# Layer one's third feed-forward group by seven half-block products, and the input sums that these need in one run behind attention's last low part

## The chip, the cores and the metric

The kernel runs on one core of a Trainium2 chip. The metric is device time in microseconds (us) of one execution. The kernel before takes 616.91 us, the median of three runs (616.11, 616.91 and 617.58). A core has five engines with queues of their own that meet through semaphores: TensorE (PE in the profile, its weight loads PEld), VectorE (DVE), ScalarE (ACT), GpSimd (POOL) and SyncE (SP, which issues most of the DMAs here).

## What is computed

Three stages follow each other; all inputs are float32. Attention over 2 batches, 8 heads and 768 tokens (a local window, and 24 block summaries) gives `x` of 1536 tokens by 512. Then two feed-forward layers:

```python
h = x @ w_in                            # 1536 x 512 x 2048
x = (h / (1 + exp(-1.702 * h))) @ w_out # 1536 x 2048 x 512
gate = 1 / (1 + exp(-(x @ w_gate)))     # 1536 x 512 x 1536
val = x @ w_val
out = (gate * val) @ w_out2             # 1536 x 1536 x 512
```

## The kernel before

Both layers work on three token blocks of 512 (block 0, 1, 2) and on groups of 256 hidden features (two halves `f` of 128): eight groups in layer one, six in layer two. Each float32 operand of a matmul is kept as two parts, a high one rounded to the matmul's type and a low one with the rest (`xH`, `xL` for the tokens, `w..H`, `w..L` for weights, `gh`, `gl` for the gated hidden block). One product of such numbers takes three matmuls: low by high, high by low, high by high. A product over the 512 input features is so 12 matmuls of 128 x 128 by 512 columns, a half of it, over 256 features (`product`, L190), is 6.

A group has a first part (`x` by its columns of `w_in`, then the gate) and a second part (the gated block by its rows of `w_out`, `second`, L541: 24 matmuls for one token block in four quarters of six, each quarter added to an accumulator `acc` by VectorE, L575). The first part comes in three forms. `first` (L517) takes one token block straight, 2 x 12 matmuls at L489. `single` (L467) takes block 2 with half products at L197. `pair` (L402) takes blocks 0 and 1 together. There the two halves `f` and the two halves of the input features make a 2 by 2 matrix of weight blocks, the two halves of the features and the two token blocks a 2 by 2 matrix of token blocks, and their product is formed by seven block products in place of eight, in Strassen's way (Winograd's form). It needs four combinations of the weight blocks (made in `load`, L167 to L186, the tiles `ws` and `s..H`, `s..L`) and four of the token blocks (made once by `input_sums`, L248, the tiles `t1` to `t3`, and `t4`, which overwrites the low half of block 1's `xH` and `xL`). Products 5 and 6 are kept in SBUF by ScalarE (L428) and added to later ones by VectorE (L431).

`PAIRED = 3` says from which group on layer one uses `pair`. Groups 0 and 1 are done for blocks 0 and 1 inside attention, as a filler. Behind attention stand, one after the other with the second part of each step behind the first part of the next, the steps (group, block): (0, 2), (1, 2), (2, 0), (2, 1), (2, 2), (3, 2), and then `pair` of group 3, with `single` of group 4 behind it, and so on up to group 7.

Within that program order a scheduler places the instructions of each engine, except where `keep_in_program_order` holds them (the input sums do that on VectorE). The input sums are 14 VectorE instructions of 128 x 1024, handed out one by one while the steps run (`folding`). The first eight come from step (0, 2) on, the rest from step (2, 1) on. The first of them may not be placed before attention's last low part (`d_lo`, L783: `xL` of the last unit).

A weight piece of 1 MB passes through `load`: VectorE takes the words apart (`da`, `db`, L132), ScalarE rescales (`da<-da`, L140), VectorE joins (L150), ScalarE rounds to the high part (L155), VectorE subtracts to the low part (L157). Then follow, for pieces that `pair` reads, four small sums `ws` (L173), a cast (L182) and a subtraction (L184). A gated block is made by ScalarE's gelu (`sg`, L514) and cast (`gh`, L508), and GpSimd's subtraction (`gl`, L509).

Of the kernel before, what the change touches and what calls it, by code (L numbers as in the profile page):

```python
# [14 lines left out]
ALU = mybir.AluOpType  # L15
# [14 lines left out]
def attention_moe_moe2_kernel(ctx: ExitStack, tc: tile.TileContext, ins: dict, out: bass.AP):  # L30
# [5 lines left out]
    B, HP, _, S = vt.shape  # L36
# [13 lines left out]
    NTB = NT // TB  # L50
# [12 lines left out]
    xH, xL = [None] * NTB, [None] * NTB  # L63
# [36 lines left out]
    def drop(*key):  # L100
        w_free.extend(w_held.pop(key))
# [9 lines left out]
    def behind(a, b):  # L111

        tc.add_manual_dep(
            a.ins, b.ins.name,
            mybir.DependencyInfo(mybir.DependencyClass.NoSync, mybir.DependencyReason.DATA), reason="order",
        )

    def load(layer, g, i, early):
# [27 lines left out]

        after = [(1, PAIRED - 1, 2, m) for m in (0, 3)] if (layer, g, i) == (1, PAIRED + 1, 0) else []
        while after and after[0] not in added:
# [10 lines left out]
        yield  # L159
        if layer == 1 and (g < PAIRED or i == 1) or layer == 2 and i == 2:  # L160
            yield
# [26 lines left out]
    LO, HI = slice(0, KC // 2), slice(KC // 2, KC)  # L188
# [16 lines left out]
    steps = [(1, g, blk) for blk in range(2) for g in range(2)]  # L205
# [9 lines left out]

    mats = {1: [w_in, w_out], 2: [w_gate, w_val, w_out2]}
    pieces, weights, raws = [], {}, []
    PAIRED = 3
    wanted = [(1, g, i) for g in range(n1) for i in range(2)] + [(2, 0, i) for i in range(3)]
    for g in range(1, n2):  # L220
        wanted += [(2, h, i) for h, i in ((g, 0), (g - 1, 2), (g, 1)) if (h, i) != (0, 2)]
# [23 lines left out]
    def t_tile(name):  # L245
        return tp.tile([P, KC // 2, TB], F32R, tag=f"t{name}", name=f"t{name}")

    def input_sums():  # L248

        def tt(**x):
            ins = nc.vector.tensor_tensor(**x)
            tc.keep_in_program_order(ins)
            return ins

        f1, f2, f3 = (tp.tile([P, KC // 2, TB], F32, tag=f"f{n}", name=f"f{n}") for n in "123")
        h1, l1, h3, l3 = (t_tile(x) for x in ("1H", "1L", "3H", "3L"))

        def whole(to, blk, half):  # L260
            return tt(out=to, in0=xH[blk][:, half], in1=xL[blk][:, half], op=ALU.add)

        behind(whole(f1, 0, LO), live["lo"])
        yield
        whole(f3, 1, LO)
        yield
        tt(out=f1, in0=f3, in1=f1, op=ALU.subtract)
        yield
        whole(f2, 1, HI)
        yield  # L270
        tt(out=f3, in0=f2, in1=f3, op=ALU.subtract)
        nc.scalar.copy(h3, f3)
        yield
        tt(out=f2, in0=f2, in1=f1, op=ALU.subtract)
        nc.scalar.copy(h1, f1)
        yield
        tt(out=l3, in0=f3, in1=h3, op=ALU.subtract)
        yield
        tt(out=l1, in0=f1, in1=h1, op=ALU.subtract)
        yield  # L280
        h2, l2 = t_tile("2H"), t_tile("2L")
        h4, l4 = xH[1][:, LO], xL[1][:, LO]
        whole(f3, 0, HI)
        yield
        tt(out=f3, in0=f3, in1=f2, op=ALU.subtract)
        nc.scalar.copy(h4, f3)
        nc.scalar.copy(h2, f2)
        yield
        tt(out=l4, in0=f3, in1=h4, op=ALU.subtract)
        yield  # L290
        tt(out=l2, in0=f2, in1=h2, op=ALU.subtract)
        tsum.update({"1": (h1, l1), "2": (h2, l2), "3": (h3, l3), "4": (h4, l4)})
        yield
# [312 lines left out]
    with tc.manual_schedule(engines={mybir.EngineType.SP}), ExitStack() as es:  # L606
# [95 lines left out]
        live = {}  # L702
# [96 lines left out]
        for _ in range(4):  # L799
# [28 lines left out]
            out=win, in_=win, pattern=[[0, NSLOT], [1, P - W0]], compare_op=ALU.is_gt, fill=NEG,  # L828
# [3 lines left out]
            out=win, in_=win, pattern=[[0, NSLOT], [-1, P - W0]], compare_op=ALU.is_gt, fill=NEG,  # L832
# [64 lines left out]
    with tc.manual_schedule(engines={mybir.EngineType.SP}):  # L897
        places(6, "w_b")
        pool([gh_slots, gl_slots], GF + 1, "g_b")
        pool([sg_slots], 5, "sg_b")  # L900
        acc_b = ctx.enter_context(tc.tile_pool(name="acc_b", bufs=1, reuse_waits="tile"))
        tp = ctx.enter_context(tc.tile_pool(name="tp", bufs=1, reuse_waits="tile"))
        ps_a, ps_b = (
            ctx.enter_context(tc.tile_pool(name=f"ps_{x}", bufs=n, space=PSUM, reuse_waits="tile"))
            for x, n in (("a", 4), ("b", 2))
        )
        ps_f, ps_s = Slots("h", (ps_a, 4)), Slots("h", (ps_h, 2), (ps_b, 2))
        folding, sums_1 = iter(()), input_sums()

        def run(main, rest=iter(()), after=()):  # L910

            for n, _ in enumerate(main):
                pull(1)
                next(folding, None)
                for _ in range(after.count(n)):
                    next(rest, None)
            for _ in rest:
                pull(1)
                next(folding, None)

        def seconds(layer, g, *blks):
            for blk in blks:
                yield from second(layer, g, blk, g == ends[layer])

        steps = [(1, g, 2) for g in range(2)] + [(1, 2, blk) for blk in range(NTB)] + [(1, PAIRED, 2)]
        prev = None
        for step in steps:
            need((*step[:2], 0))
            run(first(*step))
            if step[2] == 2 and step[1] < PAIRED:  # L930
                drop(*step[:2], 0)
            if prev:
                need((*prev[:2], 1))
                run(second(*prev, False))
                if prev[2] == 2:
                    drop(*prev[:2], 1)
            if step == (1, 0, 2):
                folding = itertools.islice(sums_1, 8)
            elif step == (1, 2, 1):
                for _ in folding:  # L940
                    pass
                folding = sums_1
            prev = step
        top = n1 - 1

        LEAD = PAIRED + 1
        for g in range(PAIRED, n1):  # L950
            need((1, g, 0), (1, g, 0, "s"))
            for _ in folding:
                pass
            if g - 1 in (LEAD, top - 1):
                run(pair(1, g), seconds(1, g - 1, 1, 0), range(7))
                if g - 1 == LEAD:
                    drop(1, g - 1, 1)
            else:
                n = g if g <= LEAD else g - 1
                need((1, n, 1))  # L960
                run(pair(1, g), second(1, n, 2, False), (0, 2, 4, 5))
                if n < g:
                    drop(1, n, 1)
            drop(1, g, 0, "s")
            if g <= LEAD:
                drop(1, g, 0)
            need((1, g, 1))
            if g in (LEAD, top - 1):
                continue
            n = g + 1 if g < LEAD else min(g, top - 1)  # L970
            need((1, n, 0))
            run(single(1, n), seconds(1, g, 1, 0), (0, 0, 1, 1, 2, 2, 3, 3))
            if g < LEAD:
                drop(1, g, 1)
            else:
                drop(1, n, 0)
        folding = token_sums()
        run(single(1, top), second(1, top - 1, 2, False), range(4))
        drop(1, top, 0)
        drop(1, top - 1, 1)  # L980
        prev = (1, top)
        ps_f, ps_s = Slots("h", (ps_a, 4), (ps_b, 2)), Slots("h", (ps_h, 2))

        def ahead(g):
            if (2, g, 1, "s") not in weights:
                pull(1)

        for g in range(n2):
            need((2, g, 0), (2, g, 1), (2, g, 0, "s"), (2, g, 1, "s"))
            for _ in folding:  # L990
                pass
            rest = second(*prev, 2, prev[0] == 1)
            if g == 0:
                rest = itertools.chain(rest, half_sums())
            for slot, _ in enumerate(pair(2, g)):
                if g:
                    ahead(g + 1)
                elif slot > 4 and (2, 0, 2) not in weights:
                    pull(1)
                if slot % 2 or g == 0 and slot:  # L1000
                    next(rest, None)
                if g and slot % 4 == 3:
                    ahead(g + 1)
            for _ in rest:
                pass
            drop(*prev, prev[0])
            drop(2, g, 0, "s")
            drop(2, g, 1, "s")
            need((2, g, 2))
            rest = seconds(2, g, 0, 1)  # L1010
            for _ in halves(g):
                ahead(g + 1)
                next(rest, None)
                ahead(g + 1)
            for _ in rest:
                pass
            drop(2, g, 0)
            drop(2, g, 1)
            prev = (2, g)
        for _ in second(*prev, 2, True):  # L1020
            pass
# [40 lines left out]
```

## Time and profile before

| | |
|---|---|
| median of three runs | 616.91 us |
| the profiled execution, of it the span of the core | 616.49 us, 614.7 us |
| TensorE busy | 599.2 us (97%), 3348 matmuls |
| VectorE, ScalarE, GpSimd busy | 447.1 us (73%), 313.5 us (51%), 199.2 us (32%) |
| chain that ended last | PE 90%, DMA 8% |
| DMA | 58.10 MB, mean 95 GB/s |

The span runs from the first to the last instruction of the core. What lies around it, 616.49 less 614.7, is 1.79 us. The chain that ended last is followed back from the last instruction to what released it; where it runs along one engine, that engine had no free time there. A matmul's line in the timeline has a duration of 0.39 us, but matmuls overlap: what a matmul costs is the distance from its start to the start of the next.

### The profile page before, as it was taken

To read this page: it belongs to the slowest core of one execution; us is meant where nothing else is said; L and a number is where in the kernel's file an instruction comes from. 1 tells how busy PE (TensorE), PEld (TensorE's weight loads), DVE (VectorE), ACT (ScalarE), POOL (GpSimd) and SP (SyncE) were. 2 spreads that over 40 slices of the span, in tenths; PEclk is the share of its full clock that TensorE was granted. 3 is DMA by queue.
4 is the path that set the end of the run, shared out by engine and by line. 5 is a ranking of instruction groups with operands and counts; after the bars stand their busy time and mean duration, and the time that the engine had idled before them with its cause. 6 is when DMAs were issued, how large, how long until landed. Compare 5 with 4: busy or idle time off the path is not lost.

```text
span 614.7 us, 8764 instructions
## 1 busy us (share of the span) xinstructions
PE 599.2 (97%) x3348; PEld 498.3 (81%) x3348; DVE 447.1 (73%) x655; ACT 313.5 (51%) x620; POOL 199.2 (32%) x164
## 2 busy tenths in 40 slices
PE   7698999999999999999999999999999999999997
PEld 4576787788888888888888888898898898898896
DVE  6699665399929988877559889568759669777434
ACT  4788657566424645535345667635445246344230
POOL 6796685323331243413322021022022022122030
PEclk9999999999999999999999999999999999999999
DMA  9999653022301421331002023222222222100014
GB/s 301 336 297 331 234 138 70 1 70 69 136 1 68 138 68 69 101 106 60 9 0 70 0 69 101 105 69 69 69 69 69 68 69 70 68 2 1 0 51 155
DMA packets 25161, 58.10 MB, mean 95 GB/s; under 512 B 1568, under 2 KB 1824, under 8 KB 25120
## 3 DMA queue, kind: packets, MB, share of 16 engines
q1 hardware_dynamic: 24400, 56.24, 28.3%
q10 hardware_dynamic: 720, 1.31, 0.6%
q8 instruction: 26, 0.43, 0.3%
q14 instruction: 15, 0.12, 0.1%
HBM read 53.08 MB, written 3.15 MB: 91 GB/s over the span
## 4 chain that ended last, share of the span: by engine, by line
PE 90%; DMA 8%; DVE 0%; POOL 0%; SPq 0%; issue 0%; ACTq 0%; POOLq 0%
PE ps_o L489 37%; PE ps_y L197 16%; PE ps_x L197 10%; PE ps_v L197 10%; PE ps_h L489 8%; PE ps_h L197 4%; DMA q<-in_q 3%; PE ps_s L710 2%; DMA vt<-in_vt 2%; PE ps_x L762 2%; DMA vwin<-in_v 1%; DMA k<-in_k 1%; PE ps_p L743 1%; PE ps_s L708 0%; POOL kx L699 0%; POOL gl L509 0%
## 5 line engine op out<-in xcount | busy, mean ns | idle before, releaser
L509 POOL TENSOR_TENSOR gl<-sg,gh 128x512 fp32r<-128x512 f32 x84 | 125.6, 1501 | 377.2 <-ACT gh L508 290.0
L575 DVE TENSOR_TENSOR acc<-ps_o,acc 128x512 f32<-128x512 f32 x143 | 96.4, 684 | 66.5 <-PE ps_o L489 66.3
L489 PE MATMUL ps_o<-gl,w_1H 128*128 128x512 f32 x192 | 75.2, 393 | 0.3 <-POOL gl L509 0.3
L489 PE MATMUL ps_o<-gh,w_1H 128*128 128x512 f32 x192 | 74.7, 390 | 0.0
L489 PE MATMUL ps_o<-gh,w_1L 128*128 128x512 f32 x192 | 71.9, 395 | 1.5 <-ACT gh L508 1.4
L508 ACT CAST gh<-sg 128x512 fp32r<-128x512 f32 x84 | 51.6, 621 | 31.3 <-DVE sg L500 24.9
L489 PE MATMUL ps_o<-w_2L,gh 128*128 128x512 f32 (+1 forms) x146 | 56.6, 387 | 0.0
L489 PE MATMUL ps_o<-w_2H,gh 128*128 128x512 f32 (+1 forms) x146 | 56.4, 386 | 0.0
L489 PE MATMUL ps_o<-w_2H,gl 128*128 128x512 f32 (+1 forms) x146 | 56.3, 389 | 0.1
L150 DVE SCALAR_TENSOR_TENSOR da<-da,db 128x1024 uint32<-128x1024 uint32 x34 | 46.9, 1379 | 9.6 <-ACT da L140 9.0
L140 ACT ACTIVATE da<-da 128x1024 f32<-128x1024 f32 x34 | 36.1, 1061 | 24.1 <-DVE da L132 21.9
L489 PEld LDWEIGHTS ps_o<-gh,w_1L 128*128 128x128 f32 x192 | 35.9, 188 | 9.3 <-ACT gh L508 2.0
L489 PEld LDWEIGHTS ps_o<-gl,w_1H 128*128 128x128 f32 x192 | 36.1, 188 | 7.6 <-POOL gl L509 0.5
L489 PEld LDWEIGHTS ps_o<-gh,w_1H 128*128 128x128 f32 x192 | 36.1, 188 | 7.3
L699 POOL TENSOR_SCALAR kx<-k 128x384 f32<-128x384 f32 x24 | 33.0, 1375 | 20.0 <-DMA k<-in_k 10.9
L723 ACT ACTIVATE e<-ps_s,nm 128x128 f32<-128x128 f32 x96 | 34.3, 381 | 9.1 <-DVE nm L715 8.0
L489 PEld LDWEIGHTS ps_o<-w_2H,gh 128*128 128x128 f32 x146 | 27.4, 188 | 5.7
L489 PE MATMUL ps_h<-xL,w_0H 128*128 128x512 f32 x80 | 31.4, 393 | 0.3 <-DVE xL L783 0.3
L489 PEld LDWEIGHTS ps_o<-w_2L,gh 128*128 128x128 f32 x146 | 27.5, 188 | 5.1
L132 DVE TENSOR_SCALAR db<-raw 128x1024 uint32<-128x1024 uint32 x33 | 30.8, 933 | 1.1 <-DMA raw<-in_moe_w_out 0.7
L489 PEld LDWEIGHTS ps_o<-w_2H,gl 128*128 128x128 f32 x146 | 27.4, 188 | 5.2 <-DVE acc L575 0.3
L489 PE MATMUL ps_h<-xH,w_0L 128*128 128x512 f32 x80 | 31.5, 403 | 0.0
(244 smaller groups left out, 1482.1 us busy)
## 6 DMA issues: line engine op xcount, KB each, us to landing
raw<-in_moe_w_out SPq DMA_DIRECT2D x13, 1024.0 KB, 4.9
raw<-in_moe_w_in SPq DMA_DIRECT2D x8, 1024.0 KB, 7.5
raw<-in_moe_w_gate SPq DMA_DIRECT2D x6, 1024.0 KB, 5.0
raw<-in_moe_w_val SPq DMA_DIRECT2D x6, 1024.0 KB, 5.0
q<-in_q SPq DMA_DIRECT2D x20, 256.0 KB, 9.4
vwin<-in_v SPq DMA_DIRECT2D x6, 768.0 KB, 9.6
k<-in_k SPq DMA_DIRECT2D x8, 400.0 KB, 7.7
out<-acc SPq DMA_DIRECT2D x11, 256.0 KB, 2.0
```

Of the source, the lines that this page charges most:

```text
L132: ins = nc.vector.tensor_scalar(**x)
L140: nc.scalar.activation(af, af, AF.Prelu, scale=REBIAS, alpha=-2.0 ** 32)
L150: ins = nc.vector.scalar_tensor_tensor(out=a, in0=a, scalar=3, in1=b, op0=ALU.logical_shift_left, op1=ALU.bitwise_or)
L197: nc.tensor.matmul(ps, lhsT=a[x][:, kk, :], rhs=b[y][:, kk, :], start=start and i == 0, stop=i == n - 1, skip_group_check=True,)
L489: nc.tensor.matmul(ps, lhsT=a, rhs=b, start=i == 0, stop=i == n - 1)
L508: nc.scalar.copy(gh, sg)
L509: nc.gpsimd.tensor_tensor(out=gl, in0=sg, in1=gh, op=ALU.subtract)
L575: added[layer, g, blk, m] = nc.vector.tensor_tensor(out=a[:, m, :], in0=ps, in1=a[:, m, :], op=ALU.add)
L699: nc.gpsimd.tensor_scalar(out=to, in0=x, scalar1=scale, scalar2=None, op0=ALU.mult)
L710: nc.tensor.matmul(ps[:, j, :], lhsT=t[:, j, :], rhs=kt[:, j, :], start=False, stop=j == G - 1)
L723: nc.scalar.activation(e[:, j, :], s[:, j, :], AF.Exp, bias=nm[:, j:j + 1], accum_out=sm[:, j:j + 1])
L762: nc.tensor.matmul(ps[64 * e:64 * e + 64, j, :], lhsT=x[:, h * D:(h + 1) * D], rhs=y[:, j, 64 * e:64 * e + 64], start=n == 0, stop=n == le ...
```

## The change

`PAIRED` goes from 3 to 2. Group 2's blocks 0 and 1 are no longer computed by `first`; they are computed by `pair`, and the steps behind attention are (0, 2), (1, 2), (2, 2) and then `pair` of group 2, with the second part of (2, 2) in it, then `single` of group 3 with the second parts of group 2's blocks 1 and 0. `LEAD`, which moves the second part of block 2 in the loop, stays 4. The weight piece (2, 0) now gets its four sums too. The input sums come one after the other from step (0, 2) on, without the pause after eight, and each of the four that read `xH` and `xL` may not be placed before attention's last low part.

```diff
@@ -215,7 +215,7 @@
-    PAIRED = 3
+    PAIRED = 2
@@ -258,9 +258,9 @@
         def whole(to, blk, half):
-            return tt(out=to, in0=xH[blk][:, half], in1=xL[blk][:, half], op=ALU.add)
-
-        behind(whole(f1, 0, LO), live["lo"])
+            behind(tt(out=to, in0=xH[blk][:, half], in1=xL[blk][:, half], op=ALU.add), live["lo"])
+
+        whole(f1, 0, LO)
         yield
         whole(f3, 1, LO)
         yield
@@ -922,7 +922,7 @@
-        steps = [(1, g, 2) for g in range(2)] + [(1, 2, blk) for blk in range(NTB)] + [(1, PAIRED, 2)]
+        steps = [(1, g, 2) for g in range(2)] + [(1, PAIRED, 2)]
@@ -935,10 +935,6 @@
             if step == (1, 0, 2):
-                folding = itertools.islice(sums_1, 8)
-            elif step == (1, 2, 1):
-                for _ in folding:
-                    pass
                 folding = sums_1
             prev = step
@@ -946,7 +942,7 @@
-        LEAD = PAIRED + 1
+        LEAD = PAIRED + 2
```

TensorE, right behind the second part of step (1, 2), in the kernel before (`ps_o_1881` is the last quarter of that second part, `ps_h_1890` the first part of block 1 of group 2):

```order
L489 MATMUL ps_o_1881<-gh1_1_2_1_1749,w1_1_1H_849 128x512
L489 MATMUL ps_h_1890<-xH1_765,w1_2_0L_1680 128x512
L489 MATMUL ps_h_1890<-xL1_766,w1_2_0H_1679 128x512
L489 MATMUL ps_h_1890<-xH1_765,w1_2_0H_1679 128x512
L489 MATMUL ps_h_1890<-xH1_765,w1_2_0L_1680 128x512
L489 MATMUL ps_h_1890<-xL1_766,w1_2_0H_1679 128x512
L489 MATMUL ps_h_1890<-xH1_765,w1_2_0H_1679 128x512
```

The same place now (`ps_x_1904` is product 1 of group 2, `gh1_2_2_0` and `gl1_2_2_0` the gated block 2 of group 2, half 0):

```order
L489 MATMUL ps_o_1892<-gh1_1_2_1_1749,w1_1_1H_849 128x512
L197 MATMUL ps_x_1904<-xH0_321,w1_2_0L_1680 128x512
L197 MATMUL ps_x_1904<-xL0_322,w1_2_0H_1679 128x512
L197 MATMUL ps_x_1904<-xH0_321,w1_2_0H_1679 128x512
L197 MATMUL ps_x_1904<-xH0_321,w1_2_0L_1680 128x512
L197 MATMUL ps_x_1904<-xL0_322,w1_2_0H_1679 128x512
L197 MATMUL ps_x_1904<-xH0_321,w1_2_0H_1679 128x512
L489 MATMUL ps_o_1915<-gh1_2_2_0_1824,w1_2_1L_1804 128x512
L489 MATMUL ps_o_1915<-gl1_2_2_0_1825,w1_2_1H_1803 128x512
L489 MATMUL ps_o_1915<-gh1_2_2_0_1824,w1_2_1H_1803 128x512
L489 MATMUL ps_o_1915<-gh1_2_2_1_1847,w1_2_1L_1804 128x512
L489 MATMUL ps_o_1915<-gl1_2_2_1_1848,w1_2_1H_1803 128x512
```

The 24 matmuls of block 0 and the 24 of block 1 are gone from the first form; product 1 with 6 matmuls stands here, the other six products follow between the second parts, and the gated block 2 of group 2 is now read 126 matmuls behind the first one of step (0, 2).

VectorE, up to the piece (3, 0) being taken apart (`da` from `raw1_3_0`), in the kernel before:

```order
L253 TENSOR_TENSOR f2_1727<-f2_1727,f1_1726 128x1024
L157 TENSOR_TENSOR w1_2_1L_1776<-da_1773,w1_2_1H_1775 128x1024
L253 TENSOR_TENSOR t3L_1732<-f3_1728,t3H_1731 128x1024
L253 TENSOR_TENSOR t1L_1730<-f1_1726,t1H_1729 128x1024
L132 TENSOR_SCALAR da_1854<-raw1_3_0_1703 128x1024
L150 SCALAR_TENSOR_TENSOR da_1854<-da_1854,db_1855 128x1024
```

and now:

```order
L253 TENSOR_TENSOR t1L_1730<-f1_1726,t1H_1729 128x1024
L253 TENSOR_TENSOR f2_1727<-f2_1727,f1_1726 128x1024
L253 TENSOR_TENSOR t3L_1732<-f3_1728,t3H_1731 128x1024
L132 TENSOR_SCALAR db_1886<-raw1_3_0_1703 128x1024
L157 TENSOR_TENSOR w1_2_1L_1804<-da_1801,w1_2_1H_1803 128x1024
L253 TENSOR_TENSOR f3_1728<-xH0_321,xL0_322 128x1024
L253 TENSOR_TENSOR t2L_1864<-f2_1727,t2H_1863 128x1024
L132 TENSOR_SCALAR da_1885<-raw1_3_0_1703 128x1024
L575 TENSOR_TENSOR acc1_2_1755<-ps_o_1854,acc1_2_1755 128x512
L150 SCALAR_TENSOR_TENSOR da_1885<-da_1885,db_1886 128x1024
```

Between attention's last low part and this `da` stood 16 instructions, the `da` counted; now there are 20. The four that came in are `s1_2_0L`, the `db` of the piece (2, 1), the sum of block 0's high half, and `t2L`.

ScalarE, around the rescaling of that `da`, in the kernel before:

```order
L140 ACTIVATE da_1854<-da_1854 128x1024
L571 COPY acc1_2_1755<-ps_o_1780 128x512
L571 COPY acc1_2_1755<-ps_o_1793 128x512
L155 CAST w1_3_0H_1856<-da_1854 128x1024
L514 ACTIVATE sg_1818<-ps_h_1805 128x512
L508 CAST gh1_2_0_0_1820<-sg_1818 128x512
```

and now:

```order
L571 COPY acc1_2_1755<-ps_o_1793 128x512
L140 ACTIVATE da_1885<-da_1885 128x1024
L514 ACTIVATE sg_1822<-ps_h_1809 128x512
L508 CAST gh1_2_2_0_1824<-sg_1822 128x512
L514 ACTIVATE sg_1845<-ps_h_1832 128x512
L508 CAST gh1_2_2_1_1847<-sg_1845 128x512
L155 CAST w1_3_0H_1887<-da_1885 128x1024
```

The rescaling stands ahead of the gelus of the block behind it in both; what moved is that this block is now block 2 of group 2.

## Rows read from the trace of the kernel before

**Rows 1.** The page: the span, TensorE's busy row, its granted clock in 40 slices.

```profile
span 614.7 us, 8764 instructions
PE 599.2 (97%) x3348; PEld 498.3 (81%) x3348; DVE 447.1 (73%) x655; ACT 313.5 (51%) x620; POOL 199.2 (32%) x164
PEclk9999999999999999999999999999999999999999
```

**Rows 2.** Busy time by windows behind attention: window, its length, engines, clock, DMA.

```profile
127.00:154.00 27.00, 27.00 (x121) 22.34 (x119) 24.84 (x25) 18.86 (x26) 8.38 (x5) 1.00 0.23 78
154.00:186.00 32.00, 32.00 (x143) 26.51 (x142) 19.79 (x24) 10.96 (x16) 10.63 (x7) 1.00 0.19 66
186.00:219.00 33.00, 33.00 (x147) 27.36 (x146) 29.17 (x38) 18.83 (x27) 9.21 (x6) 1.00 0.30 98
219.00:252.00 33.00, 33.00 (x147) 27.32 (x147) 28.88 (x37) 15.38 (x23) 8.27 (x6) 1.00 0.27 94
252.00:600.00 348.00, 348.00 (x1765) 297.53 (x1764) 249.76 (x340) 163.77 (x256) 77.54 (x52) 1.00 0.17 54
```

**Rows 3.** The chain that ended last: start, length, engine, tile, matmuls.

```profile
126.96 10.88 PE ps_h L489 x48
...
200.17 2.04 PE ps_h L197 x9
```

**Rows 4.** TensorE's timeline: start, duration; first matmuls of steps (0, 2) and (2, 1).

```profile
126.80 0.39 PE L489 MATMUL ps_h<-xH,w_0L 128*128 128x512 f32 x1
...
154.00 0.39 PE L489 MATMUL ps_h<-xH,w_0L 128*128 128x512 f32 x1
```

**Rows 5.** VectorE's timeline behind attention's last low part.

```profile
124.81 1.22 DVE L253 TENSOR_TENSOR f<-xH,xL 128x1024 f32<-128x1024 f32 x1
...
135.82 1.79 DVE L132 TENSOR_SCALAR db<-raw 128x1024 uint32<-128x1024 uint32 x1
...
138.66 2.31 DVE L157 TENSOR_TENSOR w_1L<-da,w_1H 128x1024 fp32r<-128x1024 f32 x1
...
142.03 2.30 DVE L253 TENSOR_TENSOR t1L<-f,t1H 128x1024 fp32r<-128x1024 f32 x1
144.26 0.68 DVE L132 TENSOR_SCALAR da<-raw 128x1024 f32<-128x1024 f32 x1
...
148.00 0.42 DVE L173 TENSOR_TENSOR ws<-ws,da 128x256 f32<-128x256 f32 x1
...
151.60 1.21 DVE L184 TENSOR_TENSOR s_0L<-ws,s_0H 128x1024 fp32r<-128x1024 f32 x1
...
156.90 1.21 DVE L253 TENSOR_TENSOR t2L<-f,t2H 128x1024 fp32r<-128x1024 f32 x1
```

**Rows 6.** ScalarE's timeline, same stretch.

```profile
144.97 1.06 ACT L140 ACTIVATE da<-da 128x1024 f32<-128x1024 f32 x1 [2.97 <-DVE da L132]
...
148.28 0.59 ACT L514 ACTIVATE sg<-ps_h 128x512 f32<-128x512 f32 x1
148.91 0.62 ACT L508 CAST gh<-sg 128x512 fp32r<-128x512 f32 x1
```

**Rows 7.** GpSimd's timeline, same stretch.

```profile
135.28 1.76 POOL L509 TENSOR_TENSOR gl<-sg,gh 128x512 fp32r<-128x512 f32 x1 [1.61 <-ACT gh L508]
...
141.10 2.15 POOL L509 TENSOR_TENSOR gl<-sg,gh 128x512 fp32r<-128x512 f32 x1 [1.21 <-ACT gh L508]
...
154.04 2.38 POOL L509 TENSOR_TENSOR gl<-sg,gh 128x512 fp32r<-128x512 f32 x1 [2.92 <-ACT gh L508]
158.30 1.30 POOL L509 TENSOR_TENSOR gl<-sg,gh 128x512 fp32r<-128x512 f32 x1 [1.88 <-ACT gh L508]
```

**Rows 8.** Timelines of VectorE and TensorE in attention, where piece (2, 0) is joined.

```profile
71.53 0.66 DVE L748 COPY pt<-ps_p 128x512 f32<-128x512 f32 x1
72.67 0.82 DVE L132 TENSOR_SCALAR db<-raw 128x1024 uint32<-128x1024 uint32 x1 [0.48 <-DMA raw<-in_moe_w_out]
...
74.73 0.45 PE L762 MATMUL ps_x<-pt,vwin 128*64 128x64 f32 x6
```

## The prediction, made before the changed kernel ran

> **What bounds the kernel now.** I read the page first, then the busy time by windows, then the chain, then the timelines of four engines around the end of attention. The page gives TensorE 599.2 of 614.7 us, with the granted clock at its upper level, 2.4 GHz, throughout [rows 1, 2]. The windows show where the missing 15.5 us are not: from 127 to 600 us each window is busy for its whole length [rows 2]. VectorE comes next, with 24.84 of 27 us, then 19.79 of 32, 29.17 of 33 and 28.88 of 33 us [rows 2]; it is full in stretches, but TensorE never stands still for it there. So behind attention the end is set by the number of matmuls and their pitch, and a change can gain there only by issuing fewer.
>
> The pitch: 48 matmuls at L489 take 10.88 us, 0.2267 us each; 9 half products at L197 take 2.04 us, again 0.2267 us [rows 3]. A timeline row's duration (0.39 us, [rows 4]) is no price, since neighbours overlap.
>
> **What the change removes.** Group 2 of layer one for blocks 0 and 1: 2 halves x 2 blocks x 12 matmuls = 48 before. Now seven products x 6 matmuls = 42. All are 128 x 128 by 512 columns. 6 x 0.2267 = 1.36 us. The second parts, block 2 and all other groups keep their matmuls. As TensorE is never idle from 127 to 600 us, nothing else can be won there; the gain is 1.36 us or less.
>
> The Trainium skill, "TensorE: Matmul & The Clock Gate", section Back-to-back issue gap, puts the isolated warm gap at N / 2.4 + 2.5 ns, 216 ns for 512 columns. By it the six matmuls are 1.30 us; the rows here say 0.2267 us, and the measurement decides.
>
> **What it adds off TensorE.** VectorE gets four small sums `ws` of 128 x 256 at 0.42 us, one subtraction `s_2_0L` at 1.21 us [rows 5], and two additions to kept products of 512 elements, each under the 1.22 us of a 1024-element one. ScalarE gets one cast of 1024 elements, two copies that keep products 5 and 6 and one that starts product 1's other bank, each under the 1.06 us of the rescaling [rows 6]. GpSimd does the same subtractions as before. SyncE issues the same DMAs in the same order. All of it lies beside TensorE, so it costs nothing as long as no matmul waits. I go through the places where one could.
>
> *Inside attention.* On TensorE, ScalarE and GpSimd the order there is the same up to the last unit. On VectorE the four `ws` come in where piece (2, 0) is joined, two ahead of the copy `pt` and two behind it, and a `db` of 0.82 us goes out. `pt` ended at 71.53 + 0.66 = 72.19 us; the two put it at 73.03. The matmul that reads it started at 74.73 [rows 8]. Cover 1.7 us: cost nothing. If that cover were gone, the most it could cost is the added 4 x 0.42 - 0.82 = 0.86 us.
>
> *The input sums.* Number the matmuls from the first of step (0, 2), at 126.80 us; number 120 starts at 126.80 + 120 x 0.2267 = 154.00, and the row is there [rows 4]. In the changed order the first matmul that needs `t1` is number 144 (159.4 us), `t2` number 156 (162.2), `t3` number 185, `t4` number 214 (175.3). On VectorE, `t1`, `t3` and `t2` all stand ahead of the `da` of piece (3, 0). Before, that `da` was the 16th instruction from 124.81 on and ended at 144.26 + 0.68 = 144.94 [rows 5]. Now it is the 20th. The four that came in: `s_2_0L` 1.21, `db` like the `da` 0.68, a sum like the first row's 1.22, `t2L` 1.21 [rows 5]: 4.32 us. It ends at 149.26. So the token sums are there 10 us or more before they are read, and the six products' inputs cost nothing.
>
> *The thin place.* The gated block 2 of group 2 is read by matmul 126 on (155.4 us); the last of its four tiles, `gl` of half 1, by matmul 130, at 156.27 us. ScalarE makes it behind the rescaling of that `da`: 149.26 + 1.06, then gelu 0.59, cast 0.62, gelu 0.59, cast 0.62 [rows 6] = 152.74, then GpSimd's subtraction, 1.30 alone and up to 2.38 in its longest row [rows 7]: 154.04 to 155.12. If the first subtraction is long too, it ends at 151.53 + 2.38 = 153.91 and the second at 156.29. Cover 2.2 us down to nothing. I take nothing as its cost, because the chain already holds every long row of before and the likely end is the first.
>
> Behind this matmul on TensorE stands everything else; a wait here is paid in full, as no later stretch has idle time to give it back.
>
> *Behind it.* Product 7 ends at matmul 191 (170.1 us). Addition, gelu, cast and long subtraction: 1.22 + 0.59 + 0.62 + 2.38 = 4.81, so 174.9; the last of these tiles is read by matmul 230, 178.9 us: cover 4.0 us. The cast of `gh` for group 3, half 1 of block 2 must wait till TensorE has read the tile that held its place, group 2's `gh` of block 0, at matmul 276 (189.4); with 0.62 and 2.38 it is there at 192.4 and is read at matmul 304 (195.7): cover 3.3 us. From group 5's second pass on TensorE's order is the same in both programs.
>
> **The sum.** Profiled execution 616.49 us, span 614.7 us, 1.79 us around it. The new span is 614.7 - 1.36 = 613.34, the execution 615.13. The profiled run lay 0.42 us under the median of 616.91, so the median is put at 616.91 - 1.36 = 615.55 us, 0.22% less.
>
> **The rivals.**
>
> *A short wait at the thin place, 616.7 us.* VectorE's rows beside GpSimd's are twice as long: `db` took 1.79 us beside the `gl` of 135.28, `t1L` 2.30 us beside that of 141.10, where such rows take 0.68 and 1.21 alone [rows 5, 7]. For: the new order puts four more sums into the stretch in which five such subtractions run. Against: the GpSimd rows are the same ones, and their price is in the 144.94 already. If two of the four are lengthened by 1.1 us each, `da` ends at 151.46, the first cast at 153.73, the first `gl` (2.38) at 156.11, the second (1.30) at 157.41: a wait of 1.14 us, net 616.91 - 1.36 + 1.14 = 616.7. The Trainium skill, "SBUF — State Buffer", section Who interferes with whom, says that a VectorE instruction with two SBUF inputs and a GpSimd one that reads SBUF exclude each other, and that the loser blocks for the whole instruction. The trace agrees: 2.30 against 1.21.
>
> *The same wait at full length, 620.0 us, slower.* All four lengthened by 1.1 and both `gl` at 2.38: `da` 153.66, first cast 155.93, `gl` 158.31 and 160.69, against 156.27: 4.42 us of wait, less 1.36: 3.06 us slower. For: each piece occurs in a row. Against: five subtractions can't lengthen three rows of before and four more. It turns slower than before from a second `gl` later than 157.63.
>
> *The gain is taken back later, 616.9 us.* TensorE comes 1.36 us earlier to something whose time is set elsewhere, as the weights' path over VectorE. For: VectorE at 29.17 and 28.88 of 33 us. Against: the DMA engines are under 0.30 busy [rows 2], and no window holds an idle time of TensorE. In the changed order the low part of piece (3, 0) stands on VectorE right behind an addition that waits for matmul 114 (152.6 us), and is first read by matmul 168 (164.9 us).
>
> That the change does not do what it says is ruled out by the order: 42 matmuls stand where 48 did.
>
> **How the numbers follow.** Forecast 0.75, short wait 0.14, long wait 0.05, taken back 0.06. About 0.2% (1.23 us) is what a measurement of this kernel can tell from no change: the three runs of before lie within 1.47 us. The forecast's 1.36 us is just beyond it, so I give it 0.66 for faster, which is 0.50, and the rest, with the short wait and the lost gain, 0.45 for no change; slower is the long wait, 0.05. The range: the forecast less 0.95 us, a little more than the 0.80 us by which the lowest run of before lies under its median, 614.6, up to the short wait and lost gain, 616.9.
>
> **What the profile would show.** Right: six matmuls fewer, TensorE busy for the whole of each window from 127 to 598 us, a span near 613.3 us, rows `ps_x`, `ps_v` and `ps_y` at L197 for group 2 from 154.0 us on, `t2L` before 149 us. Wrong, as the first two rivals have it: a wait of TensorE for `gl` (GpSimd) or `gh` (ScalarE) at matmul 126 to 130, near 156 us. Wrong, as the third: a wait of TensorE for VectorE or a DMA later on. A pitch other than 0.2267 us, or a new wait in attention before 126.8 us, would upset the sum itself.

## The result, and the profile after

The changed kernel takes 625.36 us (median of 4 runs, 624.76 to 626.07); the kernel before, run beside it, 616.95. The ratio is 1.0140, 95% interval 1.0128 to 1.0152: slower by 8.4 us, where 1.36 us less, 615.55 us, was forecast. The profiled execution took 624.76 us, its span is 623.0.

The page: span, TensorE's busy row, its granted clock in 40 slices, as in [rows 1].

```profile
span 623.0 us, 8772 instructions
PE 600.9 (96%) x3342; PEld 499.3 (80%) x3342; DVE 445.2 (71%) x662; ACT 316.1 (51%) x624; POOL 205.4 (33%) x164
PEclk9999999996999999999999999999999999999999
```

Six matmuls fewer, as predicted (3342 for 3348), yet the busy time rose by 1.7 us and one slice has a lower clock. Cut into windows (columns as in [rows 2]):

```profile
127.00:137.00 10.00, 10.00 (x46) 8.29 (x45) 10.00 (x12) 7.56 (x11) 5.10 (x1) 1.00 0.20 67
137.00:145.00 8.00, 0.58 (x3) 0.15 (x1) 6.90 (x8) 2.91 (x4) 8.00 (x2) 0.68 0.12 48
145.00:150.00 5.00, 4.93 (x12) 3.87 (x13) 0.00 (x0) 0.00 (x0) 3.72 (x4) 0.50 0.68 208
154.00:186.00 32.00, 32.00 (x143) 26.51 (x142) 25.32 (x32) 15.88 (x23) 7.81 (x5) 1.00 0.21 66
```

From 137 to 145 us TensorE all but stands; from 145 to 150 it runs at half the granted clock, 1.2 GHz, and gets 12 matmuls done where 22 fit at 0.2267 us. From 154 us on it is full again, as before. TensorE's list of waits gives the releaser, its timeline the place (as in [rows 4]; in brackets the idle time ahead and what ended it):

```profile
PE ps_o L489 <- POOL gl L509: 7.8, 2, 7.5
```

```profile
137.19 0.39 PE L489 MATMUL ps_o<-gh,w_1L 128*128 128x512 f32 x1
145.07 0.79 PE L489 MATMUL ps_o<-gl,w_1H 128*128 128x512 f32 x1 [7.49 <-POOL gl L509]
145.66 0.63 PE L489 MATMUL ps_o<-gh,w_1H 128*128 128x512 f32 x1
146.09 0.63 PE L489 MATMUL ps_o<-gh,w_1L 128*128 128x512 f32 x1
```

Step (0, 2) begins at 126.31 us, so the matmul at 145.07 is number 49, due at 126.31 + 49 x 0.2267 = 137.42. It is the first that reads the low part `gl` of block 2 in group 0, first half. GpSimd's and VectorE's timelines say why that is late:

```profile
131.90 16.82 POOL L509 TENSOR_TENSOR gl<-sg,gh 128x512 fp32r<-128x512 f32 x4 [10.88 <-ACT gh L508]
```

```profile
131.79 1.22 DVE L253 TENSOR_TENSOR f<-f,f 128x1024 f32<-128x1024 f32 x1
132.92 0.69 DVE L132 TENSOR_SCALAR db<-raw 128x1024 uint32<-128x1024 uint32 x1
133.53 1.22 DVE L253 TENSOR_TENSOR f<-f,f 128x1024 f32<-128x1024 f32 x1
134.66 1.22 DVE L150 SCALAR_TENSOR_TENSOR da<-da,db 128x1024 uint32<-128x1024 uint32 x1
...
143.21 0.69 DVE L132 TENSOR_SCALAR da<-raw 128x1024 f32<-128x1024 f32 x1
159.84 0.69 DVE L575 TENSOR_TENSOR acc<-ps_o,acc 128x512 f32<-128x512 f32 x1 [15.94 <-PE ps_o L489]
```

GpSimd starts the first of the four at 131.90 and ends it at 145.03, in the chain a piece of 13.13 us; alone it took 1.30 us, at most 2.38 [rows 7]. Meanwhile VectorE runs eleven more instructions without a pause, each at its bare length (1.22, 0.69), where in [rows 5] three of this stretch are stretched to 1.79, 2.31 and 2.30; the last ends at 143.90. The subtraction ends 1.1 us after that. In the kernel before, VectorE paused at this very place:

```profile
133.30 1.46 DVE L150 SCALAR_TENSOR_TENSOR da<-da,db 128x1024 uint32<-128x1024 uint32 x1 [0.93 <-ACT da L140]
```

```profile
132.38 1.29 POOL L509 TENSOR_TENSOR gl<-sg,gh 128x512 fp32r<-128x512 f32 x1 [10.87 <-ACT gh L508]
```

There the shift-and-or of `da` stood two instructions earlier and had to wait 0.93 us for ScalarE, and in that pause the subtraction began. In the new order the same instruction comes at 134.66, when ScalarE has been done for 1.17 us:

```profile
132.44 1.05 ACT L140 ACTIVATE da<-da 128x1024 f32<-128x1024 f32 x1
```

The sum. From the first matmul of step (0, 2) to the start of the last, TensorE takes 484.48 us before and 493.26 after: 8.78 more. The wait is 145.07 - 137.42 = 7.65; the six matmuls saved are -1.36; the rest, 2.49, is the half clock (read directly: 12 pitches from 145.07 to 150.24 take 5.17 us instead of 2.72, 2.45 more). Attention ended 0.49 earlier in this execution; 8.78 - 0.49 = 8.29, the difference of the spans.

### The profile page after: what moved, and what is told of

The parts are those of the page before. It is cut to its first block, busy times and chain, and to the rows that moved or that the text cites. A ratio compares the mean times of both kernels' runs of the same rounds, so it can differ in the third digit from the quotient of the medians.

```text
span 623.0 us, 8772 instructions
## 1 busy us (share of the span) xinstructions
PE 600.9 (96%) x3342; PEld 499.3 (80%) x3342; DVE 445.2 (71%) x662; ACT 316.1 (51%) x624; POOL 205.4 (33%) x164
## 4 chain that ended last, share of the span: by engine, by line
PE 87%; DMA 8%; POOL 3%; DVE 2%; issue 0%; ACT 0%; SPq 0%; ACTq 0%; POOLq 0%
PE ps_o L489 37%; PE ps_y L197 16%; PE ps_x L197 11%; PE ps_v L197 11%; PE ps_h L197 4%; PE ps_h L489 4%; DMA xH<-in_moe_w_out 3%; DMA k<-in_k 3%; POOL gl L509 2%; DMA vt<-in_vt 2%; PE ps_s L710 2%; PE ps_x L762 1%; PE ps_p L743 1%; DMA q<-in_q 1%; PE ps_s L708 0%
## 5 line engine op out<-in xcount | busy, mean ns | idle before, releaser
L509 POOL TENSOR_TENSOR gl<-sg,gh 128x512 fp32r<-128x512 f32 x84 | 131.8, 1576 | 380.2 <-ACT gh L508 279.8
L140 ACT ACTIVATE da<-da 128x1024 f32<-128x1024 f32 x34 | 36.1, 1061 | 20.8 <-DVE da L132 18.8
L710 PE MATMUL ps_s<-kx,q 128*128 128x128 f32 x192 | 28.5, 296 | 3.1 <-POOL kx L699 1.7
L710 PEld LDWEIGHTS ps_s<-kx,q 128*128 128x128 f32 x192 | 25.8, 205 | 6.7 <-POOL kx L699 3.2
L132 DVE TENSOR_SCALAR db<-raw 128x1024 uint32<-128x1024 uint32 x33 | 28.9, 877 | 0.5
```

Source lines behind the costliest of these rows:

```text
L132: ins = nc.vector.tensor_scalar(**x)
L140: nc.scalar.activation(af, af, AF.Prelu, scale=REBIAS, alpha=-2.0 ** 32)
L509: nc.gpsimd.tensor_tensor(out=gl, in0=sg, in1=gh, op=ALU.subtract)
L710: nc.tensor.matmul(ps[:, j, :], lhsT=t[:, j, :], rhs=kt[:, j, :], start=False, stop=j == G - 1)
```

## The experiments

Ratios below are against the kernel before on the same chip. In e1, e2, e3, e6 and e9 VectorE's order in this stretch is that of the changed kernel, but for the copy that e1 and e2 add.

**A pause in VectorE's row, early (e1) and four instructions later (e2).** The copy reads one element of the late low part, so VectorE must wait there for GpSimd. It stands ahead of the second `f<-f,f` in e1 and behind the third in e2. The edit of e1 (the lines that keep the tile in `first_gl` are left out; e2 places the same copy by `behind`):

```
+ seen = tp.tile([P, 8], F32, tag="seen", name="seen")
...
+ tc.keep_in_program_order(nc.vector.tensor_copy(out=seen[0:1, 0:1], in_=first_gl[0, 2, 0][0:1, 0:1].bitcast(F32)))
```

> The changed kernel with one instruction more: a VectorE copy of a single element of block 2's first low part (group 0, first half), put between db (132.92) and the sum f<-f,f (133.53), so that VectorE stands there until GpSimd has written that low part. The order on VectorE is else the same. Theory (GpSimd's subtraction is held off by VectorE's unbroken row): it runs in the hole, about 133.5 to 134.8, TensorE's matmul 49 (due at 137.42) finds it, and the 7.65 us of waiting and the 2.4 us of half clock go: 625.36 - 10.05 = 615.3 us. Rival (GpSimd is late for a reason of its own): VectorE stands until 145 with it, TensorE waits as long, and the sums come some 11 us late: 625 us or more.

> The same one-element copy, put four VectorE instructions later, between the sums f<-f,f (136.93) and t3L (138.07). Theory: GpSimd gets in at about 138.07 and ends at about 139.35, TensorE waits 139.4 - 137.42 = 2.0 us at matmul 49, and if the clock is not lowered for so short a pause the time is 615.3 + 2.0 = 617.3 us; with all of the half clock again, 619.7. Rival (GpSimd is late for a reason of its own): 625 us or more.

Measured: e1 619.32 us (ratio 1.0044, 1.0031 to 1.0057), e2 620.94 us (1.0066, 1.0054 to 1.0078). The wait followed the pause. In e1 TensorE has none for GpSimd. In e2 matmul 49 comes 1.91 us late, where 2.0 was worked out (the step begins at 126.14 us there, so it was due at 137.25), and the clock did not fall (window 137 to 139: 1.00):

```profile
139.16 0.50 PE L491 MATMUL ps_o<-gl,w_1H 128*128 128x512 f32 x1 [1.75 <-POOL gl L513]
```

```profile
136.76 1.22 DVE L253 TENSOR_TENSOR f<-f,f 128x1024 f32<-128x1024 f32 x1
139.13 0.14 DVE L277 COPY seen<-gl 1x1 f32<-1x1 f32 x1 [1.16 <-POOL gl L513]
```

GpSimd gets in the moment VectorE stops, wherever that is put. That refutes the rival: GpSimd was ready. But both times are some 4 us above the expected 615.3 and 617.3; e5 takes that up for e1.

**GpSimd asks later (e3, e6).** ScalarE's cast of that first high part in two pieces (e3, shown), or four (e6):

```
- nc.scalar.copy(gh, sg)
+ if to == (1, 0, 2, 0):
+     nc.scalar.copy(gh[:, FIRST], sg[:, FIRST])
+     nc.scalar.copy(gh[:, SECOND], sg[:, SECOND])
+ else:
+     nc.scalar.copy(gh, sg)
```

> The changed kernel with ScalarE's cast of block 2's first high part (group 0, first half) made as two casts of 256 columns each, so that GpSimd's subtraction is asked for 0.1 to 0.3 us later, 0.2 to 0.4 us into the VectorE sum that starts at 131.79; VectorE's order is the same to the last instruction. Theory one (what decides is the moment at which GpSimd asks; in all other cases of both traces it got in at the end of the VectorE instruction that ran): it gets in at 132.92, ends at 134.2, no wait: 615.3 us. Theory two (an unbroken row of VectorE instructions always holds GpSimd off until its end): no difference, 625.4 us.

> The changed kernel with ScalarE's cast of the first high part made as four casts of 128 columns, so that GpSimd asks some 0.3 to 0.6 us later than in the changed kernel; VectorE's order is the same. Theory one (the exact moment decides; in the sweep 21 of 160 requests were held to the end of the row, spread over all moments, the others got in at the end of the running instruction): in 7 cases of 8 no wait, 615.3 us. Theory two (this row holds GpSimd off whatever the moment): 625.4 us as with two casts.

Measured: 625.47 us (1.0148, 1.0133 to 1.0162) and 625.47 us (1.0145, 1.0130 to 1.0161). The request moved from 0.11 us into VectorE's sum to 0.20 and 0.38 us, less than was meant, and changed nothing: over these moments, it is not the moment that decides in this row.

**The moment, by itself (e4, e8).**

> A kernel by itself that leaves out the whole computation: 80 times GpSimd's 128x512 subtraction is released by a ScalarE copy that grows by 16 columns from one time to the next (about 14 ns), beside a row of six VectorE instructions of 128x1024 without a gap; then 80 times more with the second of the row a one-input instruction (0.69 us). So the moment of the request moves through a whole VectorE instruction. Theory one (the moment decides): most requests are served at the end of the running instruction, and a narrow stretch of them, near 0.1 us into an instruction, waits for the end of the row, some 4 to 6 us. Theory two (the row decides): all 160 wait for the end of the row. If all are served at once, the hold-off needs something that this row lacks.

> A kernel by itself that leaves out the whole computation: as the sweep, with a row of ten VectorE instructions, and the releasing ScalarE copy grown by one column (0.9 ns) from one time to the next, 160 times, so that the moment of the request moves through 140 ns. In the sweep the held requests lay mostly five steps (67 ns) apart. Theory one (a narrow alignment decides): held requests come in short runs of neighbouring columns at a fixed spacing, one in eight in all, and each waits for the end of the row, 10 us. Theory two (chance): held ones lie scattered without a pattern.

Measured in e4: 140 of 160 requests got in at the end of the running instruction, 20 were held to the end of the row of six (6.0 to 7.55 us; the 21 and 139 quoted in other expectations are a miscount by one, and the 10.3 us of idle that e9 quotes from the fine sweep is 9.6). That looked like the first theory. The fine sweep overturned it: with rows of ten, every second request was held, 80 of 160, while the moment moved by 0.14 us in all.

```profile
24.77 11.95 POOL L38 TENSOR_TENSOR gl<-dst,y 128x512 fp32r<-128x512 f32 x1 [9.61 <-ACT dst L37]
37.42 1.73 POOL L38 TENSOR_TENSOR gl<-dst,y 128x512 fp32r<-128x512 f32 x1 [0.71 <-ACT dst L37]
49.90 11.95 POOL L38 TENSOR_TENSOR gl<-dst,y 128x512 fp32r<-128x512 f32 x1 [10.74 <-ACT dst L37]
62.56 1.73 POOL L38 TENSOR_TENSOR gl<-dst,y 128x512 fp32r<-128x512 f32 x1 [0.71 <-ACT dst L37]
```

A held request makes VectorE wait at the end of its row, and the next request gets in; that one leaves VectorE without a stop, and the next is held. So the past counts: either GpSimd's idle time (0.71 against 10 us in the brackets) or the length of VectorE's row.

**Which of the two (e9, e10).** e9 adds one GpSimd instruction to the changed kernel:

```
+ nc.gpsimd.tensor_tensor(out=seen[:, 0:1], in0=f2[:, 0, 0:1], in1=f2[:, 0, 0:1], op=ALU.subtract)
```

> The changed kernel with one GpSimd instruction more: a subtraction of a single column (128x1) that reads the second sum (f2, written at about 126.6) and so stands halfway through the 10.9 us in which GpSimd has nothing to do ahead of block 2's first low part. VectorE's order is the same to the last instruction, and its scratch tile is 64 columns wide. Theory three (what decides is how long GpSimd was idle before it asks: held off after 10.3 us or more in the fine sweep, 80 times of 80, and after 10.9 us here in four kernels of four; after 0.6 to 6 us it got in at once in 139 of 160): the first low part is asked for after some 5 us of idle, gets in at 132.9, no wait of TensorE: about 616 us, as with the hole. Theory two (how dense VectorE's row is): 625.4 us again.

> A kernel by itself that leaves out the whole computation: 96 times GpSimd's 128x512 subtraction beside an unbroken row of VectorE two-input subtractions of 128x1024, with two things set apart: both engines are first idle for about 0, 4, 8 or 12 us, and the request then comes in the 1st, 3rd, 5th, 7th, 9th or 11th instruction of the row, which goes on for some six more; four moments within the instruction each. Theory three (idle time of GpSimd before it asks decides): held to the end of the row where idle plus the row before the request is over some 7 to 10 us, so at 12 us of idle even in the row's first instruction, and at 0 us of idle only from the 9th on. Theory two (the length of VectorE's unbroken row before the request decides): held from the 7th or 9th instruction on whatever the idle time, and never in the 1st or 3rd.

Measured: e9 625.34 us (1.0146, 1.0128 to 1.0164). The small instruction ran (first row), and the first low part was held all the same after 4.04 us of idle:

```profile
127.31 1.11 POOL L271 TENSOR_TENSOR seen<-f 128x1 f32<-128x1 f32 x1 [5.73 <-DVE f L253]
132.46 16.82 POOL L511 TENSOR_TENSOR gl<-sg,gh 128x512 fp32r<-128x512 f32 x4 [4.04 <-ACT gh L510]
```

Theory three, the idle time, falls. In e10 all 40 requests that came up to the row's 5th instruction got in (1.3 to 2.4 us), all 56 from the 6th on were held to its end (6.9 to 8.3 us), with GpSimd idle for 0.7 to 18.8 us in the first set and 6.1 to 26.8 us in the second. The one-element copy whose wait opens each row is not counted. The rows grow longer with the place of the request, but the 5th and the 6th both occur in rows of eleven, so it is not the row's whole length. Neighbours of each kind, GpSimd's rows:

```profile
131.87 1.33 POOL L26 TENSOR_TENSOR gl<-dst,y 128x512 fp32r<-128x512 f32 x1 [5.65 <-ACT dst L32]
148.12 7.69 POOL L26 TENSOR_TENSOR gl<-dst,y 128x512 fp32r<-128x512 f32 x1 [6.11 <-ACT dst L32]
```

and VectorE's running instruction at each, the 5th and the 6th of rows that began at 126.33 and 142.12:

```profile
130.86 1.22 DVE L46 TENSOR_TENSOR d<-a,b 128x1024 f32<-128x1024 f32 x1
132.00 2.28 DVE L46 TENSOR_TENSOR e<-a,b 128x1024 f32<-128x1024 f32 x1
...
147.79 1.22 DVE L46 TENSOR_TENSOR e<-a,b 128x1024 f32<-128x1024 f32 x1
148.93 1.22 DVE L46 TENSOR_TENSOR c<-a,b 128x1024 f32<-128x1024 f32 x1
```

In the first pair the instruction behind the request waits for GpSimd (2.28); in the second none does.

**Time or number, and PSUM (e12).**

> A kernel by itself that leaves out the whole computation: as the kernel of idle and row, with 4 us of idle and three other rows: two-input subtractions of 128x512 (0.6 us apart), one-input instructions of 128x1024 (0.6 us apart), and two-input subtractions of 128x1024 that take turns with 128x512 subtractions that read PSUM. With 128x1024 alone a request 5.6 us into the row got in at the end of the running instruction and one 6.05 us into it was held to the end of the row. If it is time that counts, the short ones change over near 6 us (10 instructions); if it is the number of instructions, near 3.3 us (the 6th). In the mixed row a request gets in within an instruction or two at any time if an instruction that reads PSUM lets GpSimd through, and then, for the changed kernel's row with its PSUM additions, the hold-off comes from the nine sums without one that follow the request.

Measured: in rows that begin from a stop it is the number. In both rows of short instructions the request in the 5th got in, 2.9 us into the row, and the one in the 6th, 3.44 us in, was held (4 let in and 16 held in each). In the mixed row all 32 got in, up to its 21st instruction. The 512-column row (start of the row, GpSimd's two requests):

```profile
64.00 0.68 DVE L43 TENSOR_TENSOR c<-a,b 128x512 f32<-128x512 f32 x1
...
80.83 0.68 DVE L43 TENSOR_TENSOR c<-a,b 128x512 f32<-128x512 f32 x1
```

```profile
66.86 1.34 POOL L26 TENSOR_TENSOR gl<-dst,y 128x512 fp32r<-128x512 f32 x1 [7.46 <-ACT dst L32]
84.27 7.99 POOL L26 TENSOR_TENSOR gl<-dst,y 128x512 fp32r<-128x512 f32 x1 [8.04 <-ACT dst L32]
```

The changed kernel's row fits: at 131.90 VectorE is in the 14th instruction since its last stop, and none of the eleven that follow reads PSUM or has to wait. But of the 14 only seven read SBUF alone, and those from PSUM seem not to count. In the kernel before, VectorE stops at 399.34 us; behind that stop come two instructions from PSUM and then four from SBUF alone. GpSimd asks at 403.16, in the sixth of the six, and the next is not from PSUM; yet it gets in at the end of the running one, and the pair of `ws` takes 1.86 us, where one takes 0.42 [rows 5]:

```profile
399.34 0.69 DVE L431 TENSOR_TENSOR sg<-ps_y,sg 128x512 f32<-128x512 f32 x1 [0.53 <-PE ps_y L197]
...
402.89 1.86 DVE L173 TENSOR_TENSOR ws<-da 128x256 f32<-128x256 f32 x2
```

```profile
403.16 2.73 POOL L509 TENSOR_TENSOR gl<-sg,gh 128x512 fp32r<-128x512 f32 x2 [9.80 <-ACT gh L508]
```

That reading comes from traces alone; no run tested it.

**One half of the change alone (e7).** `PAIRED = 3` with the sums not paused. The sums then overwrite half of block 1's input while group 2 still reads it, so its numbers differ, not its instructions.

> One half of the change alone: the input sums one behind the other from attention's last low part on, while group 2 is still done by three token blocks. VectorE's row behind attention is then as dense with sums, but in another order (the shift-and-or of da stands behind the sum of 131.8 and waits for ScalarE there). Theory one (the moment decides): nothing waits, 616.6 us as before. Theory two (the dense row decides): a wait of TensorE at matmul 49 of several us, 620 to 625 us.

Measured: 616.50 us (0.9994, 0.9985 to 1.0003), no wait. In this order the shift-and-or of `da` again stands where it must wait for ScalarE:

```profile
132.54 1.46 DVE L150 SCALAR_TENSOR_TENSOR da<-da,db 128x1024 uint32<-128x1024 uint32 x1 [0.94 <-ACT da L140]
```

So dense sums do no harm of themselves; it is the order that both halves together make on VectorE that has no stop. The other half alone was not run.

**Where e1's 4 us went (e5).** The scratch tile 64 columns wide instead of 8.

> The kernel of the early hole again, with the scratch tile that the one-element copy writes made 64 columns wide instead of 8. In the early hole TensorE no longer waited, but its matmuls on the folded input (ps_v<-t1H, ps_y<-t2H and so on) stood at pitches of 230 to 236 ns where the changed kernel has 225 to 228, some 4 us over the whole run, and those tiles lie behind the 32 bytes of the scratch tile. Theory (the 32 bytes moved the tiles off a 64-byte boundary and that made the reads slower): with 256 bytes the pitch is 227 ns again and the time 619.3 - 4 = 615.3 us. Rival (the slow pitch comes with the hole itself, by the order of the work on VectorE and GpSimd): 619.3 us again.

Measured: 616.14 us (0.9992, 0.9983 to 1.0001). Four matmuls in a row in e1, then the same in e5:

```profile
160.60 0.40 PE L197 MATMUL ps_v<-t1H,s_0L 128*128 128x512 f32 x1
160.83 0.39 PE L197 MATMUL ps_v<-t1L,s_0H 128*128 128x512 f32 x1
161.06 0.40 PE L197 MATMUL ps_v<-t1H,s_0H 128*128 128x512 f32 x1
161.30 0.40 PE L197 MATMUL ps_v<-t1H,s_0L 128*128 128x512 f32 x1
```

```profile
158.95 0.39 PE L197 MATMUL ps_v<-t1H,s_0L 128*128 128x512 f32 x1
159.18 0.39 PE L197 MATMUL ps_v<-t1L,s_0H 128*128 128x512 f32 x1
159.40 0.39 PE L197 MATMUL ps_v<-t1H,s_0H 128*128 128x512 f32 x1
159.63 0.39 PE L197 MATMUL ps_v<-t1H,s_0L 128*128 128x512 f32 x1
```

Three pitches take 0.70 us in e1 and 0.68 in e5; the 24 matmuls `ps_v<-t1H,s_0L` have a mean pitch of 0.2345 and 0.2265 us (e2 has the narrow tile too, and 0.2347). The stretch from the first matmul of step (0, 2) to the start of the last takes 487.21 us in e1 and 484.02 in e5: the width of a tile of which one element is used was worth 3.2 us. Only the width was changed; that it is the 64-byte boundary was not separated. Most of the 0.8 us above 615.3 lies in a new wait, for an addition that stands on VectorE behind two `ws`, which a pair of GpSimd subtractions stretched to 2.51 us together:

```profile
193.05 0.50 PE L491 MATMUL ps_o<-gh,w_1L 128*128 128x512 f32 x1 [0.62 <-DVE acc L579]
```

```profile
189.89 2.51 DVE L173 TENSOR_TENSOR ws<-da 128x256 f32<-128x256 f32 x2
192.32 0.68 DVE L579 TENSOR_TENSOR acc<-ps_o,acc 128x512 f32<-128x512 f32 x1
```

**A version that beats both (e11).**

```
- nc.gpsimd.tensor_tensor(out=gl, in0=sg, in1=gh, op=ALU.subtract)
+ (nc.vector if to[0] == 1 and to[1] < 2 and to[2] == 2 else nc.gpsimd).tensor_tensor(out=gl, in0=sg, in1=gh, op=ALU.subtract)
```

> The changed kernel with the four low parts of block 2 of groups 0 and 1 subtracted on VectorE, each between two instructions of its row, instead of on GpSimd; the order is else the same but for one swap of two neighbouring sums. Theory (GpSimd was kept out by VectorE's row, nothing else is late): the low parts come some 0.7 us after their place in the row, TensorE does not wait at matmul 49, the clock stays up, and no GpSimd instruction asks before 157, so that what follows is as in the changed kernel: 625.36 - 7.65 - 2.4 = 615.3 us. Rival (VectorE, 2.6 us busier, becomes late for the sums or for group 2's weights): 616.5 us or more.

Measured: 615.24 us, median of 12 runs, against 616.63; ratio 0.9983, 0.9969 to 0.9997: 0.17% faster than before, with an interval that just leaves out no change, and 10 us faster than the changed kernel. On VectorE the low part takes 0.68 us, and TensorE is full (a window as in [rows 2]). GpSimd's next subtraction came at 147.92 us and not after 157, and took its bare 1.30 us. The first low part, then the window:

```profile
133.96 0.68 DVE L509 TENSOR_TENSOR gl<-sg,gh 128x512 fp32r<-128x512 f32 x1
```

```profile
127.00:154.00 27.00, 27.00 (x121) 22.36 (x120) 23.60 (x27) 17.16 (x25) 2.58 (x2) 1.00 0.24 78
```

From the first matmul of step (0, 2) to the start of the last: 483.12 us, 1.36 less than before.

## Why the prediction was wrong

**Right:** the gain. Six matmuls of 0.2267 us were to be worth 1.36 us; with the new wait removed, e11 gives 1.36 on TensorE's timeline and 615.24 us for the predicted 615.55. Right too that a wait behind attention is paid in full, that no other place waits, and that `t1` to `t4` are early.

**The step that failed:** "GpSimd does the same subtractions as before", put at nothing "as long as no matmul waits", and with it the bounds of a subtraction, "1.30 alone and up to 2.38 in its longest row". One of them measured 13.1 us, and TensorE waited 7.65 us for it. The walk through the places where a matmul could wait left this one out: it takes up the sums and group 2's gated block, and not the gated blocks of steps (0, 2) and (1, 2), which were there before. I took the longest row of before as the worst case, though in before VectorE had paused 0.93 us just where the first subtraction ran. Both bounds came from rows in which VectorE stops now and then; the new order has a stretch without a stop. I had counted what the reordering adds to VectorE, and not what it removes from it, an idle time that another engine used.

**The rivals:** both waits were put at matmul 126 to 130, near 156 us. The wait came at matmul 49. "The GpSimd rows are the same ones, and their price is in the 144.94 already" was the argument against them; VectorE's rows were in fact not lengthened at all, because GpSimd lost. VectorE even ended its row early (143.90 for the predicted 149.26), at GpSimd's expense; so `t2L` came before 149 us, as forecast, by a mechanism that the sum did not have. The 0.05 given to a slower kernel by a wait for `gl` named other matmuls, 77 or more later, and a price put together from rows of before.

**The page:** I quoted the Trainium skill, "SBUF — State Buffer", section Who interferes with whom, that the loser blocks for the whole instruction, and said that the trace agreed. (The page writes this of VectorE's two-port modes, and calls the shared ports an exclusive lock for all.) That two SBUF inputs keep GpSimd out is what e10 shows too, and the mixed row of e12 agrees that an instruction with one SBUF input, outside those modes, lets GpSimd through. But the loser may block for much longer than an instruction: for the running one and eleven more here, to the end of the row in 188 requests of the separate kernels.

**The second term that I lacked:** a stop of 7.65 us also cost 2.49 us of half clock; one of 1.91 us (e2) cost none.

**Open:** what in VectorE makes the sixth instruction the turning point. The runs show the count, not its cause, and the count is not the whole rule. In e4, 85 requests came at one and the same place: behind the sum that the last subtraction had made wait stood four sums, the one-element copy and the sum then running. 68 of them got in and 17 were held. So near the turning point something else decides as well, which no run separated.

## What to carry to other kernels

Before an order on VectorE is made denser, look for the pauses in it that GpSimd's work runs in, and check whether a result that GpSimd owes soon falls into a stretch of more than five instructions with neither a wait nor a PSUM input. Beside such a stretch a short operation that is needed soon is better put into the row on VectorE itself (0.68 us here) than on GpSimd (13.1 us). A bound taken from the rows of before holds only while the conditions of those rows hold.

## What the hardware showed that I had not expected

- In rows that begin from a stop and have no PSUM input, a GpSimd subtraction asked for in the sixth VectorE instruction or later was held until VectorE stopped: 88 of 88 requests in e10 and e12, against 0 of 48 up to the fifth. How long GpSimd was idle (0.7 to 26.8 us) made no difference. With every second instruction from PSUM none of 32 was held.
- A scratch tile of 32 instead of 256 bytes per partition, in the pool of the folded inputs, went with a higher pitch of matmuls that read these: 0.2345 against 0.2265 us in the mean of 24 (e1 against e5), 3.2 us in all.
